# Sparse attention followed by a squared-ReLU MLP: exponentials become the stationary operand of the second attention product

## The chip, the core and the metric

The kernel runs on one core of a Trainium2 chip. The core has a matrix engine (TensorE; "PE" in the profile, and "PEld" for its weight loads), a vector engine (VectorE, "DVE"), a scalar engine for activation functions (ScalarE, "ACT"), a general engine (GpSimd, "POOL") and a sync engine ("SP") that here only issues DMA transfers. The metric is the device time of one execution in microseconds (us). The median of three runs of the kernel before is 309.66 us, from 307.91 to 309.68.

A matrix product on TensorE has two operands. The stationary one is loaded into the array by a weight load (LDWEIGHTS); its columns become the rows (partitions) of the result. The moving one is then streamed through, and its columns become the columns of the result. The result is summed up in PSUM[...].

## The reference, cut to what matters

There are 4 batches, 8 heads, 768 positions and 64 numbers per head. A query block of 32 positions sees its neighbours, the first and last block, and three drawn blocks; all else is masked. The heads of one position, put side by side, are the 512 inputs of the MLP.

```python
scores = scale * np.matmul(q, k.transpose(0, 1, 3, 2))
scores = np.where(mask, scores, -1000000000.0)
scores = scores - np.max(scores, axis=-1, keepdims=True)
attn = np.exp(scores)
attn = attn / (np.sum(attn, axis=-1, keepdims=True) + 1e-09)
out = np.matmul(attn, v)
# ... heads side by side: x is (3072, 512)
h = x @ w_in               # (512, 2048)
r = np.maximum(h, 0.0)
return (r * r) @ w_out     # (2048, 512)
```

## The kernel before

Two heads form a pair, u, so there are 16 of them, four for each batch. Queries are taken 256 at a time (qi, three of them) and keys 256 at a time (cp, three of them). One step of attention is therefore (u, qi, cp), and there are 16 x 3 x 3 = 144 steps. Scores are computed transposed, with keys on the partitions and queries along the row; ACT takes the exponential of 1024 of them per partition in one instruction; DVE multiplies by the mask (116 steps; in the first 28 the mask is added in the scores by TensorE).

The second product has the values as its stationary operand. Each of the two value tiles has 64 columns of one head and 64 columns of ones, so the result holds, by feature, the sum over the values in one half of the partitions and the sum of the exponentials, 64 times over, in the other half:

```python
def values(u, qi, cp):
    ...
    otile[u, qi] = pool.tile([P, 2, QW], F32, name="po", tag=tag)      # QW = 256
    for c in range(2):
        nc.tensor.matmul(po[:, 0, :], VA[i][:, n, :], pT[:, 0, c, :], start=first, stop=last, ...)
        nc.tensor.matmul(po[:, 1, :], VB[i][:, n, :], pT[:, 1, c, :], start=False, stop=last, ...)
```

When the three cp of a (u, qi) are in, the sums are inverted, by ACT as exp(-ln(sum)) for 44 of the 48, by DVE for four, and DVE multiplies. The result already lies by feature, as the MLP needs it (xT):

```python
def inverse(u, qi, on="ACT"):
    ...
        nc.scalar.activation(out=ls[0:D, :], in_=po[D:P, 0, :], func=AF.Ln)
        nc.scalar.activation(out=ls[D:P, :], in_=po[0:D, 1, :], func=AF.Ln)
        nc.scalar.activation(out=rs, in_=ls, func=AF.Exp, scale=-1.0)
    # ... or on DVE: two copies and a reciprocal

def normalize(u, qi):
    ...
    V.tensor_mul(out=xT[b][0:D, a, qsl], in0=po[0:D, 0, :], in1=rs[0:D, :])
    V.tensor_mul(out=xT[b][D:P, a, qsl], in0=po[D:P, 1, :], in1=rs[D:P, :])
```

The MLP takes 256 positions at a time in the first batch and 384 in the others. Its first product (hidden, tile ph) is followed by ReLU on DVE or ACT and squaring on GpSimd, its second (output, tile py) by a copy and a store:

```python
def hidden(T, f, half):      # w is 256 or 384 positions
    ...
        nc.tensor.matmul(ph, w_in_sb[:, kc, f * P:(f + 1) * P], xT[b][:, kc, c0:c0 + w], ...)
def output(T, ts, part):
    ...
        nc.tensor.matmul(py, gtile[T, f][:, ts * P:(ts + 1) * P], w_out_sb[:, f, :], ...)
```

The order of all this on the engines is fixed when the program is built. A small scheduler in the kernel holds a list of tasks, each with an engine (or a choice of two), a cost in us written by hand, a priority, what it waits for and what buffer it takes; it plays them through and writes each engine's instructions in the order in which they came out. At run time each engine works off its own list in order. The MLP of one batch is mixed in this way into the attention of the next.

```python
va = Task("PE", 0.44, k + 2.2, (lambda a=a: values(*a)), deps=[mm] + cv[u] + va_all[-1:], ...)
if cp == CP - 1:
    on = {"ACT": (1.2, k - 9)}
    if u < HP and qi < NQ_REC:
        on["DVE"] = (2.6, k - 9)
    inv = Task(on, 0, 0, (lambda *on, u=u, qi=qi: inverse(u, qi, *on)), deps=[va], **SEM)
    mu[u, qi] = Task("DVE", 0.87, k - 9, (lambda u=u, qi=qi: normalize(u, qi)), deps=[inv], ...)
```

Of the kernel before, what the change touches and what calls it, by code (L numbers as in the profile page):

```python
# [19 lines left out]
P = 128  # L20
# [5 lines left out]
def kernel(  # L26
# [8 lines left out]
    out: bass.AP,  # L35
):


# [141 lines left out]

    sb_i = consts.tile([nb, n_rand * 2], I32, name="sb_i")
    nc.sync.dma_start(out=sb_i, in_=sampled_blocks.bitcast(I32))
    load_part(nc.scalar, 0, 1, 0, 1)
    load_part(nc.scalar, 0, 0, 0, 1)
    load_part(nc.sync, 0, 1, 1, CP)
# [10 lines left out]
    V, G = nc.vector, nc.gpsimd  # L196
    QT, KT, VA, VB = [], [], [], []
    NPB = 5
    for i in range(NPB):
        QT.append(consts.tile([P, S], BF, name=f"QT{i}"))  # L200
        KT.append(consts.tile([P, S], BF, name=f"KT{i}"))
        VA.append(consts.tile([P, NCH, P], BF, name=f"VA{i}"))
        VB.append(consts.tile([P, NCH, P], BF, name=f"VB{i}"))

    def init_v(eng, i):
        eng.memset(VA[i][:, :, D:P], 1.0)
        eng.memset(VB[i][:, :, 0:D], 1.0)

# [35 lines left out]
    def one_hot_b(n0, n1):  # L244
        cols = slice(n0 * P, n1 * P)
        V.tensor_copy(out=oh[HALVES[1], cols], in_=oh[HALVES[0], cols])
# [14 lines left out]
                    op0=AOP.min, op1=AOP.min)  # L261
    V.memset(oh[HALVES[0], 2 * P:], 1.0)
    V.memset(pm[:, 0, 0:1], 0.0)
    V.memset(pm[:, 0, nb - 1:nb], 0.0)
    one_hot(2, NCH)
    bm = consts.tile([nb, 2, D], BF, name="bm")
# [7 lines left out]
    V.scalar_tensor_tensor(out=bm[:, :, 0:nb], in0=pm[:, 1:2, :].broadcast_to([nb, 2, nb]), scalar=NEG,  # L274
                           in1=pm[:, 0:1, :].broadcast_to([nb, 2, nb]), op0=AOP.mult, op1=AOP.mult)


# [35 lines left out]
    def cast_v(u, h):  # L313
        dst = VB[u % NPB][:, :, D:P] if h else VA[u % NPB][:, :, 0:D]
        G.tensor_copy(out=dst, in_=raw[u][2][:, h])  # L315

# [7 lines left out]

    def evac(u, w, c0, c1):
        dst = (KT if w else QT)[u % NPB]
        cols = slice(c0 * 2 * P, c1 * 2 * P)
        V.tensor_copy(out=dst[:, cols], in_=ptp.pop((u, w, c0))[:, cols])

# [27 lines left out]
    added = set()  # L357
    ptile, stile, otile, rtile, xT = {}, {}, {}, {}, {}

# [31 lines left out]
    def values(u, qi, cp):  # L391
        i = u % NPB
        pT = ptile.pop((u, qi, cp))
        if cp == 0:
            pool, tag = (ps_y, "y") if o_pool(u, qi) == "y" else (ps_o, "po")
            otile[u, qi] = pool.tile([P, 2, QW], F32, name="po", tag=tag)
        po = otile[u, qi]
        for c in range(2):
            n = cp * 2 + c
            first, last = n == 0, n == NCH - 1  # L400

            nc.tensor.matmul(po[:, 0, :], VA[i][:, n, :], pT[:, 0, c, :],  # L402
                             start=first, stop=last, skip_group_check=True)
            nc.tensor.matmul(po[:, 1, :], VB[i][:, n, :], pT[:, 1, c, :],  # L404
                             start=False, stop=last, skip_group_check=True)

    def inverse(u, qi, on="ACT"):
        po = otile[u, qi]
        ls = work.tile([P, QW], F32, name="ls", tag="ls")
        rs = work.tile([P, QW], F32, name="rs", tag="rs")  # L410
        if on == "ACT":
            nc.scalar.activation(out=ls[0:D, :], in_=po[D:P, 0, :], func=AF.Ln)  # L412
            nc.scalar.activation(out=ls[D:P, :], in_=po[0:D, 1, :], func=AF.Ln)  # L413
            nc.scalar.activation(out=rs, in_=ls, func=AF.Exp, scale=-1.0)  # L414
        else:
            V.tensor_copy(out=ls[0:D, :], in_=po[D:P, 0, :])
            V.tensor_copy(out=ls[D:P, :], in_=po[0:D, 1, :])
            V.reciprocal(out=rs, in_=ls)
        rtile[u, qi] = rs

    def normalize(u, qi):
        b, a = divmod(u, HP)
        if b not in xT:
            xT[b] = consts.tile([P, HP, S], BF, name=f"xT{b}")
        po, rs = otile.pop((u, qi)), rtile.pop((u, qi))
        qsl = slice(qi * QW, (qi + 1) * QW)
        V.tensor_mul(out=xT[b][0:D, a, qsl], in0=po[0:D, 0, :], in1=rs[0:D, :])  # L427
        V.tensor_mul(out=xT[b][D:P, a, qsl], in0=po[D:P, 1, :], in1=rs[D:P, :])  # L428

# [74 lines left out]
    NQ_Y = 2  # L504
    NQ_REC = 2
    KR, KY = 0, 500
# [3 lines left out]
    K_PARTS = {0: [(0, 1), (1, CP)]}  # L510
    land_k = [(3.1, 4.7), (6.3,), (9.5,), (12.0,)]
    land_q = [(3.7, 15.0, 16.5), (6.8, 15.4, 16.9), (9.9, 15.8, 17.3), (12.4, 16.2, 17.7)]
    land_v = [8.4, 11.0, 13.5, 14.6]
# [19 lines left out]
    wu[-1].put.append(wu[0].bufs[0])  # L533
    oh_t = Task("DVE", 0.2, 0.3, (lambda: one_hot_b(2, NCH)), after=4.2, **SEM)
    for i in range(HP):
        Task("POOL", 0.8, 0, (lambda i=i: init_v(G, i)), after=4.5 + 2.6 * i)
    rc = []
    for qi in range(NQ):
        rp = Task("PE", 0.107, -7 if qi == 0 else 6 * qi - 6, (lambda qi=qi: rows_product(qi)), get="h",
                  deps=[oh_t] if qi else [], after=4.0 if qi == 0 else 7.0 * qi, **pe)  # L540
        rc.append(Task({"ACT": (0.37, -7 if qi == 0 else 300), "DVE": (0.3, 6 * qi - 6)}, 0, 0, (lambda on, qi=qi: rows_copy(qi, on)), deps=[rp], put=[rp], **SEM))
    for qi in range(NQ):
        for cp in range(CP):
            k = (qi - NQ_ADD) % NQ * CP + cp
            s = HP * CP * (NQ_ADD + k // CP) + k % CP - 6
            t = Task("PE", 0.27, s, (lambda a=(qi, cp): mask_product(*a)), deps=[rc[qi]],
                     get="h", after=20.0 + 2.0 * k if k < 3 else 52.0 + 2.0 * k, **pe)
            mk[qi, cp] = Task("DVE", 0.62, s, (lambda a=(qi, cp): mask_copy(*a)), deps=[t], put=[t], **SEM)

    def prepare_first(u):  # L550
# [4 lines left out]
        for w, c0, c1, at, s in parts:  # L555
            n = c1 - c0
            a = (u, w, c0, c1)
            on = "POOL" if c0 and not w else "ACT" if u == 0 and not c0 else "DVE"
            c = Task(on, 0.06 + {"DVE": 0.17, "POOL": 0.36, "ACT": 0.31}[on] * n, s - 6,
                     (lambda a=a, e={"DVE": V, "POOL": G, "ACT": nc.scalar}[on]: cast_qk(e, *a)), get="qc", after=at, **SEM)  # L560
            t = Task("PE", 0.15 * n, s - 5 - w, (lambda a=a: transp(*a)), deps=[c], get="h", put=[c], **pe)
            e = Task("DVE", 0.06 + 0.17 * n, s - 5, (lambda a=a: evac(*a)), deps=[t], put=[t], **SEM)
            tr[u].append(c)
            for i in range(c0, c1):
                ev[u][w, i] = e
# [9 lines left out]
    def prepare(u):  # L575
# [17 lines left out]
        if u < NPB:  # L593
            early = [Task("POOL", 0.8, s0 - 8, (lambda u=u: init_v(G, u)), after=29.0, **SEM)]
        cv[u] = [Task("POOL", 0.6, s0 - 12, (lambda u=u, h=h: cast_v(u, h)), deps=[ld_t] + old_va + early, **SEM)
# [10 lines left out]
    def attend(s, slots):  # L606
        sc = Task("PE", 0.645 if len(slots) > 1 else 0.56 if s < N_ADD else 0.42, s, (lambda: scores(slots)),
                  deps=[t for u, qi, cp in slots if (u, qi, cp) in added for t in (rc[qi], oh_t)[:1 + (cp > 0)]] + [ev[u][1, cp] for u, qi, cp in slots] + [ev[u][0, qi] for u, qi, cp in slots] + sc_all[-1:],
                  get="ps", n=len(slots), **pe)
        sc_all.append(sc)  # L610
        for j, a in enumerate(slots):
# [4 lines left out]
            if a not in added:  # L616
                mm = Task("DVE", 0.82, k - 1, (lambda a=a: mask_mul(V, *a)), deps=[ex, mk[qi, cp]], **SEM)
            va = Task("PE", 0.44, k + 2.2, (lambda a=a: values(*a)), deps=[mm] + cv[u] + va_all[-1:],
                      get=None if cp else o_pool(u, qi), put=[ex], **pe)
# [3 lines left out]
            if cp == CP - 1:  # L623
                on = {"ACT": (1.2, k - 9)}
                if u < HP and qi < NQ_REC:
                    on["DVE"] = (2.6, k - 9)
                inv = Task(on, 0, 0, (lambda *on, u=u, qi=qi: inverse(u, qi, *on)), deps=[va], **SEM)
                mu[u, qi] = Task("DVE", 0.87, k - 9, (lambda u=u, qi=qi: normalize(u, qi)), deps=[inv],
                                 put=[va_all[-CP]], **SEM)

# [14 lines left out]
    for k, T in enumerate(TILES + [None]):  # L645
# [4 lines left out]
        for _, kind, x in sorted(both, key=lambda e: e[:2]):  # L650
# [14 lines left out]
            else:  # L665
# [12 lines left out]
                elif part == NY - 1:  # L678
# [3 lines left out]

    run_schedule({"PE": 3.3, "DVE": 3.9, "ACT": 3.1, "POOL": 4.4, "SP": 10.5},
                 {"ps": 2, "po": 1, "h": 2, "y": 1, "pT": PT_BUFS, "r": R_BUFS, "g": G_BUFS, "ys": 3,
                  "qc": QC_BUFS}, ring={"SP": 16.0, "POOL": 14.0})

# [29 lines left out]
```

The softmax here doesn't subtract the row's maximum and nothing guards it: scores larger than these inputs give would overflow.

## Time and profile before

| | before |
|---|---|
| median of three runs | 309.66 us |
| span of the profiled run | 306.4 us |
| TensorE matmuls | 2308, busy 97% of the span |
| VectorE | 393 instructions, busy 72% |
| ScalarE | 344 instructions, busy 71% |
| GpSimd | 226 instructions, busy 58% |
| granted TensorE clock | 1.00 |
| DMA | 34.47 MB, 112 GB/s in the mean |

The profile comes as a page with six parts: busy time of each engine; the span in 40 slices; the DMA queues; the chain of work that ended last; groups of instructions with their count, total and mean time and the idle time in front of them; and DMA issues. Further views list instructions in order of time, or the busy time of every engine in stretches of the span.

One thing has to be known to read the TensorE rows. Matmuls are pipelined: the time of one in a group ("mean ns") runs from its start to its end in the array, and the next one starts long before that. What a matmul costs is the distance from its start to the next one's start, and this is read from the list in order of time.

In slices, the run has three stages: from 7 to 37 us there is attention alone; from 37 to 260 us attention and MLP together; from 260 us to the end MLP alone.

### The profile page before, as it was taken

Reading aid. Unit: us, or ns where it says so; the run is one execution under the profiler, and the core shown is the slowest. Engines: PE = TensorE matmul, PEld = TensorE weight load, DVE = VectorE, ACT = ScalarE, POOL = GpSimd, SP = SyncE. Lnnn points to the kernel's source line nnn. Section 1 sums busy time; section 2 is a strip of 40 time slices with the busy share of each in tenths; the row PEclk is TensorE's granted clock in tenths of the full one; section 3 lists DMA queues with packets and bytes.
Section 4 is the critical chain, followed back from the end, with each engine's and each line's share of the span. In section 5 each row is a group of like instructions: output and inputs, shape, how many; then the busy total and the mean of one; then the engine's idle time right before and its main releaser. Section 6 shows DMA issues by size and latency. Waiting matters only on the chain.

```text
span 306.4 us, 6104 instructions
## 1 busy us (share of the span) xinstructions
PE 298.0 (97%) x2308; PEld 175.8 (57%) x2308; DVE 221.4 (72%) x393; ACT 218.8 (71%) x344; POOL 177.2 (58%) x226
## 2 busy tenths in 40 slices
PE   6999999999999999999999999999999999999995
PEld 4665656656766665555565555555655656555542
DVE  8778888698998878897767677767767866544521
ACT  3899999777978887888888888788888886200000
POOL 5680388765795576977444395755435345566620
PEclk9999999999999999999999999999999999999999
DMA  6997999735717167557001266501000000100002
GB/s 211 350 203 132 312 160 178 195 91 178 214 27 214 38 207 206 111 157 216 34 0 37 70 198 202 100 1 36 34 0 36 1 36 34 36 35 34 36 37 100
DMA packets 42597, 34.47 MB, mean 112 GB/s; under 512 B 20680, under 2 KB 39624, under 8 KB 42568
## 3 DMA queue, kind: packets, MB, share of 16 engines
q1 hardware_dynamic: 37656, 29.50, 34.1%
q0 software_dynamic: 4224, 4.19, 8.6%
q10 hardware_dynamic: 688, 0.39, 0.4%
q8 instruction: 18, 0.29, 0.4%
q14 instruction: 11, 0.09, 0.1%
HBM read 27.26 MB, written 6.29 MB: 109 GB/s over the span
## 4 chain that ended last, share of the span: by engine, by line
PE 85%; DVE 6%; ACT 4%; DMA 2%; issue 1%; POOL 0%; SPq 0%; ACTq 0%; DVEq 0%
PE py L471 25%; PE ph L444 24%; PE po L402 11%; PE ps L373 10%; PE po L404 9%; PE ps L369 3%; ACT pT L379 2%; DVE pT L384 2%; DMA ks<-in_k_dram 2%; PE pq L294 1%; PE pt L321 1%; DVE r L452 1%; DVE xT L428 1%; DVE xT L427 1%; ACT ls L413 1%
## 5 line engine op out<-in xcount | busy, mean ns | idle before, releaser
L458 POOL TENSOR_TENSOR g<-r 128x384 bf16<-128x384 f32 (+1 forms) x144 | 133.1, 935 | 89.1 <-DVE r L452 69.9
L379 ACT ACTIVATE pT<-ps 128x1024 bf16<-128x1024 f32 x144 | 142.4, 1019 | 16.3 <-PE ps L373 15.8
L384 DVE TENSOR_TENSOR pT<-pT,mask 128x1024 bf16<-128x1024 bf16 x116 | 93.1, 814 | 23.5 <-ACT pT L379 21.7
L444 PE MATMUL ph<-xT,w_in_sb 128*128 128x384 bf16 (+1 forms) x576 | 106.1, 308 | 0.1
L471 PE MATMUL py<-w_out_sb,g 128*128 128x512 bf16 x384 | 104.2, 379 | 0.5 <-ACT ys L478 0.5
L444 PEld LDWEIGHTS <-w_in_sb 128*128 128x128 bf16 x576 | 54.8, 98 | 38.6 <-issue 4.5
L402 PE MATMUL po<-pT,VA 128*128 128x256 bf16 x288 | 68.8, 274 | 0.9 <-DVE xT L428 0.7
L452 DVE TENSOR_SCALAR r<-ph 128x384 f32<-128x384 f32 (+1 forms) x96 | 48.8, 510 | 27.1 <-PE ph L444 17.2
L404 PE MATMUL po<-pT,VB 128*128 128x256 bf16 x288 | 68.2, 273 | 0.0
L471 PEld LDWEIGHTS <-g 128*128 128x128 bf16 x384 | 36.6, 98 | 29.0 <-issue 3.2
L373 PE MATMUL ps<-QT,KT 64*128 64x256 bf16 x576 | 46.8, 271 | 0.3 <-ACT pT L379 0.3
L402 PEld LDWEIGHTS <-VA 128*128 128x128 bf16 x288 | 28.0, 97 | 19.0 <-issue 10.2
L373 PEld LDWEIGHTS <-KT 64*128 64x128 bf16 x576 | 23.2, 94 | 21.0 <-issue 17.6
L404 PEld LDWEIGHTS <-VB 128*128 128x128 bf16 x288 | 28.2, 98 | 5.4 <-issue 0.9
L450 ACT ACTIVATE r<-ph 128x384 f32<-128x384 f32 (+1 forms) x48 | 21.9, 456 | 12.5 <-PE ph L444 10.8
L478 ACT COPY ys<-py 128x512 f32<-128x512 f32 x15 | 8.7, 580 | 28.9 <-PE py L471 28.9
L427 DVE TENSOR_TENSOR xT<-po,rs 64x256 bf16<-64x256 f32 x48 | 19.7, 410 | 9.8 <-ACT rs L414 9.5
L412 ACT ACTIVATE ls<-po 64x256 f32<-64x256 f32 x44 | 16.8, 381 | 11.1 <-PE po L404 10.2
L309 POOL CAST qc<-qs 128x768 bf16<-128x768 f32 (+1 forms) x20 | 15.2, 767 | 10.4 <-DMA qs<-in_q_dram 9.1
L428 DVE TENSOR_TENSOR xT<-po,rs 64x256 bf16<-64x256 f32 x48 | 20.5, 428 | 0.6
L414 ACT ACTIVATE rs<-ls 128x256 f32<-128x256 f32 x44 | 18.3, 417 | 1.4
L315 POOL CAST VA<-vs 128x384 bf16<-128x384 f32 x16 | 9.3, 584 | 15.2 <-DMA vs<-in_v_dram 9.5
(57 smaller groups left out, 123.9 us busy)
## 6 DMA issues: line engine op xcount, KB each, us to landing
vs<-in_v_dram SPq DMA_DIRECT2D x16, 384.0 KB, 5.0
out_dram<-ys SPq DMA_DIRECT2D x23, 256.0 KB, 2.1
ks<-in_k_dram SPq DMA_DIRECT2D x15, 384.0 KB, 4.3
qs<-in_q_dram SPq DMA_DIRECT2D x12, 384.0 KB, 3.6
w_in_sb<-in_moe_w_in_dram POOLq DMA_DIRECT2D x4, 512.0 KB, 8.0
w_out_sb<-in_moe_w_out_dram POOLq DMA_DIRECT2D x4, 512.0 KB, 11.1
qs<-in_q_dram SPq DMA_DIRECT2D x11, 128.0 KB, 5.1
ks<-in_k_dram SPq DMA_DIRECT2D x1, 256.0 KB, 4.0
```

Of the source, the lines that this page charges most:

```text
L373: nc.tensor.matmul(ps[:, h, c, :], KT[i][hs, ksl[c]], QT[i][hs, qsl], start=not add, stop=True, skip_group_check=True)
L379: nc.scalar.activation(out=pT, in_=stile.pop((u, qi, cp)), func=AF.Exp, scale=scale)
L384: eng.tensor_mul(out=pT, in0=pT, in1=mask[:, None, qi, cp * 2:cp * 2 + 2, :].broadcast_to([P, 2, 2, QW]))
L402: nc.tensor.matmul(po[:, 0, :], VA[i][:, n, :], pT[:, 0, c, :], start=first, stop=last, skip_group_check=True)
L404: nc.tensor.matmul(po[:, 1, :], VB[i][:, n, :], pT[:, 1, c, :], start=False, stop=last, skip_group_check=True)
L427: V.tensor_mul(out=xT[b][0:D, a, qsl], in0=po[0:D, 0, :], in1=rs[0:D, :])
L428: V.tensor_mul(out=xT[b][D:P, a, qsl], in0=po[D:P, 1, :], in1=rs[D:P, :])
L444: nc.tensor.matmul(ph, w_in_sb[:, kc, f * P:(f + 1) * P], xT[b][:, kc, c0:c0 + w], start=(kc == 0), stop=(kc == KM - 1))
L450: nc.scalar.activation(out=r, in_=htile.pop((T, f)), func=AF.Relu)
L452: V.tensor_scalar(out=r, in0=htile.pop((T, f)), scalar1=0.0, scalar2=None, op0=AOP.max)
L458: G.tensor_mul(out=g, in0=r, in1=r)
L471: nc.tensor.matmul(py, gtile[T, f][:, ts * P:(ts + 1) * P], w_out_sb[:, f, :], start=(f == 0), stop=(f == NF - 1))
```

## The change

The two operands of the second attention product change places. The exponentials, 128 queries at a time, become the stationary operand, and the values of one head with one column of ones, 65 columns in all, become the moving one. The result then lies by query: for each of its 128 partitions 64 sums of values and, in column 64, the sum of the exponentials. The division needs one number per query and head, so the inverse is a small reciprocal on DVE and no longer exp(-ln) on ACT. In exchange the result lies the wrong way round for the MLP and has to be transposed: by TensorE for the first batch (12 of the 48 tiles, with a copy out of PSUM), by a DMA transpose for the others (36). The purpose is to stream fewer columns through TensorE (8 x 65 in place of 4 x 256 for each step; half of the stationary columns of before were ones), and to take the inverses from ACT and the wide multiplications from DVE.

With this go smaller edits at the start: the value tiles need only two columns of ones (before 64), the loads and the one-hot tile of the mask are issued in another order, and two copies of the first tiles may run on ACT.

```diff
@@ values
-            nc.tensor.matmul(po[:, 0, :], VA[i][:, n, :], pT[:, 0, c, :],
-                             start=first, stop=last, skip_group_check=True)
-            nc.tensor.matmul(po[:, 1, :], VB[i][:, n, :], pT[:, 1, c, :],
-                             start=False, stop=last, skip_group_check=True)
+            for h in range(2):
+                for j in range(QW // P):
+                    nc.tensor.matmul(po[:, j, h, :], pT[:, h, c, j * P:(j + 1) * P], VV[i][:, n, h, 0:D + 1],
+                                     start=n + h + j == 0, stop=n == NCH - 1, skip_group_check=True)
@@ inverse, normalize
-            nc.scalar.activation(out=ls[0:D, :], in_=po[D:P, 0, :], func=AF.Ln)
-            nc.scalar.activation(out=ls[D:P, :], in_=po[0:D, 1, :], func=AF.Ln)
-            nc.scalar.activation(out=rs, in_=ls, func=AF.Exp, scale=-1.0)
...
-        V.tensor_mul(out=xT[b][0:D, a, qsl], in0=po[0:D, 0, :], in1=rs[0:D, :])
-        V.tensor_mul(out=xT[b][D:P, a, qsl], in0=po[D:P, 1, :], in1=rs[D:P, :])
+        V.reciprocal(out=rs, in_=po[:, :, D])
+        V.tensor_tensor(out=xn, in0=po[:, :, 0:D], in1=rs[:, :, None].broadcast_to([P, QW // P * 2, D]), op=AOP.mult)
@@ new
+    def x_transp(u, qi):
+        xn = xtile.pop((u, qi)).rearrange("p (j h) d -> p j (h d)", h=2)
+        pt = ps_h.tile([P, QW], BF, name="px", tag="h")
+        for j in range(QW // P):
+            nc.tensor.transpose(pt[:, j * P:(j + 1) * P], xn[:, j, :], identb)
+    def x_evac(u, qi, on):
+        (nc.scalar.copy if on == "ACT" else V.tensor_copy)(out=x_to(u, qi), in_=xtile.pop((u, qi)))
+    def x_dma(u, qi):
+        nc.sync.dma_start(out=x_to(u, qi).rearrange("r (n p) -> r n p", p=P),
+                          in_=xtile.pop((u, qi)).rearrange("p g d -> p (g d)"), transpose=True)
@@ attend
-            va = Task("PE", 0.44, k + 2.2, (lambda a=a: values(*a)), deps=[mm] + cv[u] + va_all[-1:],
+            va = Task("PE", 0.42, k + 2.2, (lambda a=a: values(*a)), deps=[mm] + cv[u] + va_all[-1:],
...
+                nm = Task("DVE", 0.55, k - 9, (lambda u=u, qi=qi: normalize(u, qi)), deps=[va],
+                          get="xn", put=[va_all[-CP]], **SEM)
+                if u < HP:
+                    xp = Task("PE", 0.12, k - 9, (lambda u=u, qi=qi: x_transp(u, qi)), deps=[nm], ...)
+                    mu[u, qi] = Task({"DVE": (0.3, k - 9), "ACT": (0.37, k - 9)}, 0, 0, ... x_evac ...)
+                else:
+                    mu[u, qi] = Task("SP", 1.3, k - 9, (lambda u=u, qi=qi: x_dma(u, qi)), deps=[nm],
+                                     put=[nm], late=2.0, dma=0.4)
```

## The prediction

> **What bounds the kernel now.** I read the page's busy times and chain of waits first, then the groups, then the busy times of the three stages, and last the matmuls in order of time.
>
> ```profile
> PE 298.0 (97%) x2308; PEld 175.8 (57%) x2308; DVE 221.4 (72%) x393; ACT 218.8 (71%) x344; POOL 177.2 (58%) x226
> ...
> PE 85%; DVE 6%; ACT 4%; DMA 2%; issue 1%; POOL 0%; SPq 0%; ACTq 0%; DVEq 0%
> ```
>
> TensorE is the bound: 85% of the chain that ended last. The three stages, each with the busy time of every engine:
>
> ```profile
> 7.00:37.00 30.00, 29.62 (x341) 18.78 (x337) 23.61 (x50) 27.49 (x36) 13.09 (x28) 1.00 1.00 248
> 37.00:260.00 223.00, 221.19 (x1724) 132.55 (x1722) 174.78 (x293) 185.18 (x297) 138.50 (x158) 1.00 0.42 106
> 260.00:302.00 42.00, 42.00 (x222) 21.61 (x221) 17.00 (x30) 3.42 (x7) 21.11 (x26) 1.00 0.12 45
> ```
>
> After the length come PE, PEld, DVE, ACT and POOL. In the first stage ACT is full too (27.5 of 30); in the middle one DVE stands at 78% and ACT at 83%; the last is TensorE alone. The groups that the change touches:
>
> ```profile
> L384 DVE TENSOR_TENSOR pT<-pT,mask 128x1024 bf16<-128x1024 bf16 x116 | 93.1, 814 | 23.5 <-ACT pT L379 21.7
> L402 PE MATMUL po<-pT,VA 128*128 128x256 bf16 x288 | 68.8, 274 | 0.9 <-DVE xT L428 0.7
> L404 PE MATMUL po<-pT,VB 128*128 128x256 bf16 x288 | 68.2, 273 | 0.0
> L427 DVE TENSOR_TENSOR xT<-po,rs 64x256 bf16<-64x256 f32 x48 | 19.7, 410 | 9.8 <-ACT rs L414 9.5
> L412 ACT ACTIVATE ls<-po 64x256 f32<-64x256 f32 x44 | 16.8, 381 | 11.1 <-PE po L404 10.2
> L414 ACT ACTIVATE rs<-ls 128x256 f32<-128x256 f32 x44 | 18.3, 417 | 1.4
> ```
>
> A matmul's 274 ns is its passage, not its cost. The cost is the distance between starts, here from the list in order of time, TensorE's matmuls and then two of its weight loads:
>
> ```profile
> 11.12 0.27 PE L402 MATMUL po<-pT,VA 128*128 128x256 bf16 x1
> 11.23 0.27 PE L404 MATMUL po<-pT,VB 128*128 128x256 bf16 x1
> 11.34 0.61 PE L321 MATMUL pt<-identb,qc 128*128 128x128 bf16 x8
> 11.78 0.27 PE L402 MATMUL po<-pT,VA 128*128 128x256 bf16 x1
> ```
>
> ```profile
> 9.05 0.11 PEld L321 LDWEIGHTS <-qc 128*128 128x128 bf16 x2 [0.21 <-issue]
> ```
>
> A value product of 256 columns costs 0.11 us (11.12 to 11.23; over a run of twelve it is 0.109). Eight transposes of 128 columns, each with a new full stationary operand, take from 11.34 to 11.78, 0.055 us each (0.056 where the starts are read one by one). And two weight loads, each 0.10 long by itself, fit in 0.11 us: the second starts some 0.015 us after the first. So a weight load holds up the stream far less than its own duration says.
>
> **What the Trainium skill says.** (1) "TensorE: Matmul & The Clock Gate", section "LDWEIGHTS (loading the stationary operand)", gives columns / 1.2 ns, 107 ns for 128 columns. The record agrees as a duration (97 to 98 ns) but not as a cost: pairs of load and product run here every 56 ns. (2) The same page, "Back-to-back issue gap", gives columns / 2.4 + 2.5 ns for a lone product, a floor near 25 ns, and some 81 ns for each product of 128 columns in a stream of load and product pairs. The trace agrees with the first (0.109 at 256 columns, 0.056 at 128) and contradicts the 81. No run here goes below 128 columns. (3) "PSUM — Partial Sum Buffer", "Specifications (TRN2)": cache lines of 8 bytes, and patterns that aren't contiguous slow matmuls. The new results are 65 fp32 wide, so every second one starts in mid line; no run here shows what that costs. (4) "VectorE: DVE Perf Modes", "The perf-mode tier table": a two-tensor operation with an operand in PSUM runs at the lowest rate. The trace agrees: 256 elements from PSUM take 0.41 us.
>
> **The change part by part.**
>
> *Value products.* Removed: 576 x 0.109 = 62.8 us of TensorE. Added: 144 x 8 = 1152 products of 65 columns. The line through 0.109 at 256 and 0.056 at 128 has 0.41 ns per column and 3 ns fixed, 0.030 us at 65 (an estimate; the load's 0.015 hides under it): 34.6 us. Saved 28.2.
>
> *Transposes by TensorE.* 12 tiles x 2 x 0.056 = 1.3 us. Net for TensorE: -26.9.
>
> *ACT.* Off go 44 x (0.381 + 0.376 + 0.417) = 51.7 us.
>
> *DVE.* Off go 48 x (0.410 + 0.428) = 40.2, and the four inverses there, 4 x (0.426 + 0.417 + 1.752) = 10.4. On come 48 multiplications of 256 elements from PSUM at 0.42 (as the ReLU of 128x256) and 48 reciprocals of 4 elements (0.13 estimated: the smallest operations here take that, and 1752 ns for 256 leave 27 for 4), 26.4 in all, and nine copies at 0.27, 2.5. The scheduler then gives DVE 80 ReLUs of 384 in place of 63, and 27 of 256 in place of 33, net +7. DVE: about -15.
>
> *GpSimd and SP.* 36 DMA transposes come to SP. Those of Q and K, three times as large, need 1.2 us to issue and 2.9 to land; tasks after them wait in SP's order.
>
> *Where it lies.* The built instruction order says how the work is cut. Before the first hidden product there are now 54 x 4 = 216 value products of the new kind, 27 steps (before 23); behind the last value product stand 204 hidden and 200 output products (before 96 and 122). So the tail grows, and the middle must be summed anew:
> - First stage. ACT needs 27 x 1.02 = 27.5 us for its exponentials from 7.4 on and is now the bound, as TensorE falls to about 0.86 a step: scores 0.43, two switches between the 64-row scores and 128-row products at some 0.1 each, values 0.24. It ends near 37.5.
> - Middle, before 223.5 us. Off: 108 hidden at 0.163, 17.6; 78 outputs at 0.216, 16.8; 32 score products at 0.054, 1.7; values from 484 x 0.109 = 52.8 to 936 x 0.030 = 28.1, 24.7. On: 0.4. TensorE needs 163.
> - But DVE, counted in the same way over its order, needs 158 there (115 masks x 0.814 = 94, 39 divisions 21, ReLUs 27, casts 9, mask copies, stores and evacuations 7), ACT 134. Two engines with nearly the same load, in fixed orders, don't overlap fully; with 6% for waits I take 172.
> - Tail: 204 x 0.163 + 200 x 0.216 = 76.5, and 3.7 from the last product to the end as before.
> Sum 37.5 + 172 + 76.5 + 3.7 = 289.7 of span. The median was 3 us above the profiled span before: 292 us.
>
> **Rivals.** *A. A floor near 52 ns for each pair of load and product* (the load itself, the feed of instructions, or the half cache lines). For it: nothing in the trace runs below 0.055, and the new code's hand-written cost is 0.42 for eight. Against it: the two loads 0.015 apart. Then values cost 59.9, the net saving is 1.6, the middle takes about 183 and is TensorE-bound again, the first stage 40: some 304 to 306 us. *B. DVE becomes the bound of the middle stage and runs with more waits than I gave it*: it has 158 of work, and its masks (0.81 in the mean) reach 1.1 to 1.2 us beside GpSimd. At 185 for the middle: 305. *C. The detour by DMA transposes.* Each batch's MLP now waits for a landing, behind loads of 384 KB and stores in SP's order; six tiles of MLP with 2 us each would give back 12: 304. Against it: the other batches' work lies ready, and the single PSUM tile of the sums is free after one DVE step of 0.55 us, which before took 1.17 on ACT and 0.84 on DVE. *D. All hidden*: if DVE and TensorE interleave perfectly, 281.
>
> **Range and chances.** The main line, at 0.030 to 0.038 a product, I hold at two in three, with 283 to 298; A at one in five; the rest is B and C on top. Predicted 292 us, range 282 to 307. Faster by over 2% (below 303.5): 0.77; within: 0.19; slower: 0.04, as no computing engine gets more work than it sheds.
>
> **What would show it.** The distance between starts in a run of eight value products: 30 ns (right), 50 and more (A). The middle stage's busy times: DVE over 90% with TensorE waiting for masks speaks for my middle; TensorE full there speaks for A. Hidden products waiting for a DMA of xT: C. The division as 0.42 + 0.13, a tail of about 76 us behind the last value product, and the first hidden product near 37. I am wrong if the products follow at 50 ns or above, or if TensorE stands idle over 20 us in the middle.

## The result and the profile after

The change makes the kernel faster, and by about as much as was predicted: 296.31 us in the median (294.70 to 298.01 in four runs) beside 309.11 (307.91 to 309.68) for the kernel before. The ratio is 0.959, with a 95% interval from 0.952 to 0.966. The profiled span went from 306.4 to 292.8 us.

First the page of the kernel after: its busy times and the engines' shares of the chain that ended last.

```profile
PE 275.7 (94%) x2870; PEld 160.5 (55%) x2908; DVE 208.2 (71%) x400; ACT 166.8 (57%) x206; POOL 173.6 (59%) x223
...
PE 59%; DVE 20%; DMA 10%; issue 4%; ACT 2%; SPq 2%; POOL 2%; DVEq 0%; ACTq 0%; POOLq 0%
```

(38 of TensorE's 2908 matmuls, all of them output products, have no record in this trace, so its 94% is a little low.) ACT lost 52.0 us and DVE 13.2. TensorE is still the busiest engine, but its share of the chain fell from 85% to 59%, DVE's rose from 6% to 20%, and that of DMA, mostly loads of K and V, from 2% to 10%. Where this happens is seen in the busy times by stage, cut at the starts of the first hidden product, of the last value product and of the last product of all (start and end, length, then PE, PEld, DVE, ACT, POOL, granted clock, DMA share, GB/s):

```profile
7.00:39.05 32.05, 31.65 (x514) 21.04 (x513) 17.56 (x51) 28.09 (x30) 13.48 (x26) 1.00 1.03 249
39.05:212.24 173.19, 163.04 (x1939) 97.47 (x1968) 154.13 (x273) 131.24 (x163) 113.74 (x129) 1.00 0.56 139
212.24:288.37 76.13, 75.71 (x402) 39.47 (x407) 32.51 (x58) 4.11 (x7) 42.89 (x52) 1.00 0.12 43
```

In the middle stage TensorE now stands idle for 10.1 us of 173.2 (before 1.8 of 223.0), DVE is busy for 89% (before 78%), and ACT has dropped from 83% to 76%. The waits of this stage say for whom TensorE stands idle (engine, line, released by: us in total, times, longest):

```profile
PEld L402 <- DVE pT L383: 12.9, 29, 1.2
PEld L402 <- DVE xn L410: 7.7, 13, 1.3
PE po L402 <- DVE pT L383: 4.6, 14, 0.7
PE po L402 <- DVE xn L410: 2.6, 6, 0.8
```

All four are value products waiting for DVE: for a masked tile of exponentials, or for the division that frees the one PSUM tile of the sums (po). The rows of PEld and PE tell in part of the same waits and aren't added. The 10.1 us count only the time in which no matmul is on its way; where the distances between starts exceed what the products cost elsewhere, TensorE loses some 14 us in this stage (an estimate from all its starts; the same sum is about 4 before). TensorE waits for no load here; DVE waits 2.4 us and GpSimd 4.8 for loads of K and V, and what these cost the whole wasn't tested. No hidden product waits for a landing of xT; the view has no such line.

How cheap the products became is read from TensorE's instructions in order of time:

```profile
122.95 0.42 PE L402 MATMUL po<-VV,pT 128*128 128x65 bf16 x8 [0.26 <-DVE pT L383]
123.22 0.49 PE L447 MATMUL ph<-xT,w_in_sb 128*128 128x384 bf16 x2
```

Eight value products, each with its own weight load, start at 122.95, and the next group follows at 123.22: 0.27 us for eight (0.26 in the median of all steps). Within the groups the distance from one start to the next is 32 ns in the median. The 0.42 behind the start is the passage of the group: seven distances of 0.032 and the last product's own 0.194. Last, the groups that the prediction priced:

```profile
L383 DVE TENSOR_TENSOR pT<-pT,mask 128x1024 bf16<-128x1024 bf16 x116 | 99.3, 878 | 5.6 <-ACT pT L378 5.1
L402 PE MATMUL po<-VV,pT 128*128 128x65 bf16 x1152 | 58.7, 194 | 7.7 <-DVE pT L383 4.6
L410 DVE TENSOR_TENSOR xn<-po,rs 128x256 bf16<-128x256 f32 x48 | 20.4, 424 | 1.7
L409 DVE RECIPROCAL rs<-po 128x4 f32<-128x4 f32 x48 | 8.5, 176 | 9.7 <-PE po L402 9.6
```

The multiplication came as estimated (0.424 for 0.42). The masks, which the change doesn't touch, take 0.878 in place of 0.814, and the reciprocal 0.176 in place of 0.13. The same two rows give the wait that is gone: before, DVE stood 21.7 us in front of the masks for ACT's exponentials, now 5.1.

### The profile page after: what moved, and what is told of

It reads as the page before. It is cut to its first block, busy times and chain, and to the rows that moved or that the text cites. A ratio compares the mean times of both kernels' runs of the same rounds, so it can differ in the third digit from the quotient of the medians.

```text
span 292.8 us, 7241 instructions
## 1 busy us (share of the span) xinstructions
PE 275.7 (94%) x2870; PEld 160.5 (55%) x2908; DVE 208.2 (71%) x400; ACT 166.8 (57%) x206; POOL 173.6 (59%) x223
## 4 chain that ended last, share of the span: by engine, by line
PE 59%; DVE 20%; DMA 10%; issue 4%; ACT 2%; SPq 2%; POOL 2%; DVEq 0%; ACTq 0%; POOLq 0%
PE py L474 20%; PE ph L447 20%; DVE pT L383 11%; PE po L402 8%; PE ps L372 6%; DMA ks<-in_k_dram 6%; DMA vs<-in_v_dram 3%; PE ps L368 2%; DVE xn L410 2%; DVE r L455 2%; ACT pT L378 2%; DVE qc L309 2%; DVE mask L299 1%; SPq L168 1%; PE pt L320 1%
## 5 line engine op out<-in xcount | busy, mean ns | idle before, releaser
L474 PE MATMUL py<-w_out_sb,g 128*128 128x512 bf16 x346 | 97.0, 379 | 1.8 <-issue 0.2
L455 DVE TENSOR_SCALAR r<-ph 128x384 f32<-128x384 f32 (+1 forms) x107 | 55.7, 521 | 40.4 <-POOL g L461 21.0
L402 PEld LDWEIGHTS <-pT 128*128 128x128 bf16 x1152 | 47.1, 98 | 37.2 <-DVE pT L383 12.9
L402 PE MATMUL po<-VV,pT 128*128 128x65 bf16 x1152 | 58.7, 194 | 7.7 <-DVE pT L383 4.6
L372 PEld LDWEIGHTS <-KT 64*128 64x128 bf16 x576 | 23.5, 95 | 17.6 <-issue 14.2
L314 POOL CAST VV<-vs 128x384 bf16<-128x384 f32 x32 | 21.4, 698 | 13.8 <-DMA vs<-in_v_dram 12.4
L453 ACT ACTIVATE r<-ph 128x256 f32<-128x256 f32 (+1 forms) x37 | 15.9, 431 | 11.5 <-PE ph L447 10.2
L410 DVE TENSOR_TENSOR xn<-po,rs 128x256 bf16<-128x256 f32 x48 | 20.4, 424 | 1.7
L409 DVE RECIPROCAL rs<-po 128x4 f32<-128x4 f32 x48 | 8.5, 176 | 9.7 <-PE po L402 9.6
L309 DVE CAST qc<-ks 128x768 bf16<-128x768 f32 (+1 forms) x16 | 11.6, 724 | 3.5 <-DMA ks<-in_k_dram 3.5
L368 PE MATMUL ps<-bq,oh 64*128 64x256 bf16 x112 | 11.7, 288 | 0.4 <-ACT pT L378 0.4
```

What stands on the lines that cost most here:

```text
L309: (eng.copy if eng is nc.scalar else eng.tensor_copy)(out=c[:, ns], in_=raw[u][w][:, :, ns, :].rearrange("p t n d -> p n t d"))
L314: G.tensor_copy(out=VV[u % NPB][:, :, h, 0:D], in_=raw[u][2][:, h])
L368: nc.tensor.matmul(ps[:, h, c, :], oh[hs, ksl[c]], bq[hs, qsl], start=c == 0, stop=False, skip_group_check=True)
L372: nc.tensor.matmul(ps[:, h, c, :], KT[i][hs, ksl[c]], QT[i][hs, qsl], start=not add, stop=True, skip_group_check=True)
L402: nc.tensor.matmul(po[:, j, h, :], pT[:, h, c, j * P:(j + 1) * P], VV[i][:, n, h, 0:D + 1], start=n + h + j == 0, stop=n == NCH - 1, skip_ ...
L410: V.tensor_tensor(out=xn, in0=po[:, :, 0:D], in1=rs[:, :, None].broadcast_to([P, QW // P * 2, D]), op=AOP.mult)
```

## Experiments

Two theories were to be told apart. The first: the gain is TensorE's cheaper products, it needed ACT's relief as well, and what limits the middle stage now is DVE, mostly through its masks. The rival: TensorE's new pairs of load and product are still the limit, by a floor or by waits that the detour through transposes brings. All changes below are made to the kernel after, ratios are to the kernel before, and the times of stages are from the profiled run.

### Wider moving operand

```diff
-    nc.tensor.matmul(po[:, j, h, :], pT[...], VV[i][:, n, h, 0:D + 1],
+    w0 = (n * 2 + h) * (D + 2)
+    nc.tensor.matmul(po[:, j, h, :], pT[...], VV[i].rearrange("p n h d -> p (n h d)")[:, w0:w0 + P],
```

128 columns are streamed where 65 are needed; the extra ones are neighbours in the tile and aren't read (tiles are widened to hold them).

> The same kernel with 128 moving columns in place of 65 (the other 63 are streamed and never read); order and all other engines unchanged. A product should then cost 0.056 in place of 0.030 us, 1152 x 0.026 = 30 us more on TensorE, 24 of them in the middle stage. Theory 1 (the saved columns are the gain; TensorE had some 10 us of slack against DVE in the middle): middle about 173 + 14 = 187 us, first stage 41, time 313 or so, no faster than the kernel before. Theory 2 (the gain comes from the work taken from ACT and DVE, TensorE's columns hardly matter): time stays below 303.

Measured: ratio 1.006 (1.002 to 1.009), median 314.15 us of eleven runs. Six of them ran in a slower state of the chip and are not in the ratio; the other five have a median of 310.36. One step's products in order of time, and the middle stage:

```profile
101.25 0.61 PE L404 MATMUL po<-VV,pT 128*128 128x128 bf16 x8
```

```profile
42.85:229.88 187.03, 183.99 (x1969) 120.67 (x1968) 153.12 (x270) 130.96 (x163) 111.44 (x126) 1.00 0.50 125
```

The distance is 56 ns in the median, as the transposes of before had shown for 128 columns. That is 1152 x 0.024 = 28 us more for TensorE, and the span grew by 17.6: the rest fell into TensorE's waits, whose idle time shrank from 10.1 to 3.0 us in this stage. The whole gain of the change is gone, though ACT and DVE keep theirs. So the gain hangs on the products' 32 ns, and this kernel shows what a floor in the fifties would have cost.

### ACT's old work put back

```diff
+    nc.scalar.activation(out=ls[0:D, :], in_=warm[0:D, :], func=AF.Exp)
+    nc.scalar.activation(out=ls[D:P, :], in_=warm[0:D, :], func=AF.Exp)
+    nc.scalar.activation(out=lr, in_=ls, func=AF.Exp, scale=-1.0)
```

Each division is accompanied by three activations of the sizes of the old inverse, on a constant; nobody reads them. The built order doesn't know of them. They sum to 59.5 us, 7.8 more than the old inverses, since there are 48 in place of 44 and two of the three activations take longer (0.41 for 0.38).

> The change with ACT's old load put back: at each of the 48 divisions ACT runs three activations of the sizes of the old inverse on a constant tile; nothing reads them. Adds 48 x 1.17 = 56 us to ACT, 46 of them in the middle stage. Theory 1 (TensorE's columns alone are the gain, ACT had room): within 1% of the changed kernel, 296. Theory 2 (both reliefs are needed, because the steps now come faster than ACT with its inverses could serve them): ACT has 127 + 46 = 173 us in a middle of 173 and 9 to 11 us more in the first stage, so the middle goes to 180 to 185 and the time to 310 to 318, and the gain is gone.

Measured: ratio 1.011 (1.006 to 1.015), median 311.8 us. The first and the middle stage:

```profile
7.00:43.82 36.82, 31.29 (x512) 21.30 (x508) 18.14 (x54) 35.51 (x54) 15.30 (x34) 1.00 0.99 237
43.82:229.40 185.58, 168.90 (x1969) 98.26 (x1968) 150.49 (x270) 169.83 (x282) 106.01 (x126) 1.00 0.50 126
```

ACT is the fullest engine in both (35.5 of 36.8, 169.8 of 185.6), its share of the chain is 34% (2% in the kernel after), and TensorE, with its cheap products, stands idle for 16.7 us in the middle. Even if the 7.8 us are taken off in full, less than half of the gain is left. Taking work from TensorE alone would have brought little in this order or nothing; both reliefs were needed. An order planned with these activations in it wasn't tried and might do better.

### Narrower moving operand

```diff
+    d0 = 0 if n == 0 else D + 1 - 32
-    nc.tensor.matmul(po[:, j, h, :], pT[...], VV[i][:, n, h, 0:D + 1],
+    nc.tensor.matmul(po[:, j, h, d0:], pT[...], VV[i][:, n, h, d0:D + 1],
```

For all but the first of the six key tiles only 32 of the 65 columns are streamed: the sums of the other 33 features are left incomplete.

> Five of the six key tiles stream only 32 of the 65 columns of the values (the sums of the other 33 features are left incomplete); order and the other engines unchanged. Takes up to 5/6 x 1152 x 33 x 0.41 ns = 13 us from TensorE, 11 of them in the middle stage, unless a product cannot go below some 25 ns. Theory 1 (DVE bounds the middle stage): the time stays within 1% of 296. Theory 2 (TensorE's columns still set the pace, its waits are only where the order puts them): 284 to 288.

Measured: 296.16 us, ratio 0.958 (0.954 to 0.962): the time of the kernel after. One step's products, then the middle stage:

```profile
101.15 0.36 PE L403 MATMUL po<-VV,pT 128*128 128x32 bf16 x8
101.36 0.38 PE L448 MATMUL ph<-xT,w_in_sb 128*128 128x256 bf16 x2
```

```profile
38.90:212.60 173.70, 160.59 (x1969) 92.77 (x1968) 155.32 (x273) 130.94 (x163) 112.91 (x128) 1.00 0.56 139
```

The distance fell only to 25 ns in the median and 26 in the mean (0.21 for eight), so TensorE was relieved of some 960 x 0.006 = 6 us. That is less than half of what the columns would suggest, and the test is weaker for it; but these 6 us bought nothing (295.03 us in the run whose clock was 1.00, where the kernel after has 294.70 and 295.36). TensorE isn't what sets the middle stage. The Trainium skill, "TensorE: Matmul & The Clock Gate", section "Back-to-back issue gap", states an issue floor near 25 ns up to 64 columns; the 25 at 32 agrees, and its formula for a lone product gives 29.6 for 65 columns where the trace has 32. That floor lies below the change's width, and so rival A's doesn't exist at this one.

### Fewer masks

```diff
 def mask_mul(...):
+    if cp == 1:
+        return
```

39 of the 116 mask multiplications are left out; masked keys of the middle third are then counted in the output.

> The mask multiplication of DVE is left out where cp is 1 (some 39 of 116, so masked keys count there; order unchanged). Takes 39 x 0.88 = 34 us from DVE and nothing from TensorE. Theory 1 (DVE is the bound of the middle stage, 166 us busy of 173): the middle falls to what TensorE needs, 161 to 165, time 285 to 289. Theory 2 (TensorE's waits come from the fixed order and from round trips, not from DVE's load): middle stays at 171 or above, time 294 to 296.

Measured: 287.84 us, ratio 0.930 (0.925 to 0.935). The middle stage:

```profile
40.27:205.88 165.61, 161.46 (x1970) 98.93 (x1969) 122.04 (x234) 129.93 (x163) 103.06 (x129) 1.00 0.62 145
```

DVE's load in the stage fell by 32.1 us, the stage by 7.6, and then it met TensorE, which has only 4.2 us of idle time left there. DVE was the limit, but by a narrow margin.

### GpSimd made light

```diff
-    r = work.tile([P, TWM], F32, name="r", tag="r", bufs=R_BUFS)[:, 0:T[2]]
+    r = work.tile([P, TWM], BF, name="g", tag="g", bufs=G_BUFS + R_BUFS)[:, 0:T[2]]
-    G.tensor_mul(out=g, in0=r, in1=r)
+    g = rltile.pop((T, f))
+    G.tensor_mul(out=g[:, 0:32], in0=g[:, 0:32], in1=g[:, 0:32])
```

Why do the same masks take longer than before the change? In this version GpSimd squares 32 columns in place and leaves the others unsquared; the order on all engines is that of the kernel after.

> The changed kernel in its own order, with GpSimd's squaring cut to 32 of the 256 or 384 columns, in place in the tile that the ReLU writes (the other columns stay unsquared). Takes some 100 us of work from GpSimd, nothing from DVE, ACT or TensorE. Theory 1 (a mask multiplication on DVE takes longer while GpSimd works): the masks' mean falls from 0.88 to 0.76 or less, DVE has 14 us less to do in the middle stage, which shortens to 160 to 167, time 283 to 290. Theory 2 (the masks' length has nothing to do with GpSimd): mean stays at 0.85 or above and the time within 1% of 296.

Measured: 286.26 us, ratio 0.924 (0.919 to 0.929). The groups of the squares and of the masks, then the middle stage:

```profile
L460 POOL TENSOR_TENSOR g<-g 128x32 bf16<-128x32 bf16 x144 | 53.7, 377 | 139.4 <-DVE g L455 108.8
L383 DVE TENSOR_TENSOR pT<-pT,mask 128x1024 bf16<-128x1024 bf16 x116 | 82.1, 726 | 10.1 <-ACT pT L378 9.5
```

```profile
38.86:206.17 167.31, 161.77 (x1939) 100.01 (x1968) 135.98 (x273) 130.42 (x163) 67.56 (x130) 0.98 0.61 145
```

GpSimd's 173.6 us became 95.4, and DVE's 208.2 became 189.5 with no instruction fewer: its masks fell from 0.878 to 0.726, its casts of K from 0.724 to 0.592. (Its input is now a bf16 tile; the ReLUs that write it take 0.521 as before.) TensorE's weight loads wait 5.4 us for masks in place of 12.9, the middle stage is 5.9 us shorter, the span 6.1. (TensorE was granted only half its clock for 6.8 us of this stage, so without that the difference may be larger.) In the trace of the kernel after, the masks during which GpSimd was idle throughout take 0.69 us (16 of them), and those during which it worked throughout, on squares or on casts, 0.98 (36). The Trainium skill, "SBUF — State Buffer", section "Who interferes with whom", says that a DVE instruction with both inputs in SBUF contends with a GpSimd instruction that reads SBUF; the traces agree, and put a size on it.

### All transposes by TensorE

```diff
-                if u < HP:
+                if True:
```

> The 36 DMA transposes of the later batches are undone: TensorE transposes these tiles too, and DVE or ACT copies them out (16 more on DVE, 20 more on ACT), as for the first batch. Adds 36 x 2 x 0.056 = 4 us to TensorE and 16 x 0.28 = 5 us to DVE. Theory 1 (the DMA detour is hidden, DVE bounds the middle): 4 to 9 us slower than the change, 300 to 305. Theory 2 (hidden products lose time waiting for the DMA's landing): equal or faster, 290 to 296.

Measured: 296.58 us, ratio 0.960 (0.956 to 0.965). It was expected to be slower, and that was a miss. The middle stage:

```profile
39.77:211.29 171.52, 164.66 (x2022) 99.24 (x2021) 153.24 (x284) 136.59 (x184) 111.14 (x125) 1.00 0.52 125
```

The 72 further transposes and the copies out of PSUM find room (of the 48 copies ACT does 23 and DVE 25) in an order that is made anew: the middle stage is 1.7 us shorter, the tail 3.5 longer. The time is the same. So the DMA detour cost nothing that TensorE transposes would save, and saved nothing either.

### The true costs in the scheduler's book

```diff
-            va = Task("PE", 0.42, ...values...)
+            va = Task("PE", 0.24, ...values...)
```

The scheduler plans a value step at 0.42 us, as long as the passage of its eight products; 0.24 is eight times the prediction's 0.030, and the distances in the trace sum to 0.26.

> One number changed: the scheduler's cost of eight value products is 0.24 us, which is their distance from start to start, in place of 0.42, which is the passage of the eight. The order is made anew: more of the MLP goes into the middle stage (128 hidden and 146 output products behind the last value product in place of 204 and 200) and ACT gets more of the ReLUs there. Theory 1 (DVE bounds the middle, so attention can't go faster, but its waits can be filled with MLP work of TensorE): TensorE's idle time of some 20 us is used for half or more, time 282 to 290. Theory 2 (the order does not matter, DVE's load sets the end): within 1% of 296.

Measured: 292.31 us, ratio 0.945 (0.941 to 0.950). It is faster than the kernel after, but outside what was expected. The middle stage, and a stretch of DVE, GpSimd, TensorE and ACT near its start:

```profile
35.31:234.07 198.76, 192.81 (x2170) 112.49 (x2166) 166.73 (x285) 142.09 (x179) 134.91 (x151) 0.98 0.56 132
```

```profile
44.28 5.28 DVE L383 TENSOR_TENSOR pT<-pT,mask 128x1024 bf16<-128x1024 bf16 x4
...
45.77 3.24 POOL L461 TENSOR_TENSOR g<-r 128x256 bf16<-128x256 f32 x4
...
47.58 0.42 PE L402 MATMUL po<-VV,pT 128*128 128x65 bf16 x8 [1.47 <-DVE pT L383]
...
48.42 1.02 ACT L378 ACTIVATE pT<-ps 128x1024 bf16<-128x1024 f32 x1 [1.47 <-PE ps L372]
```

The tail behind the last value product is now 52.1 us in place of 76.1, so 24 us of MLP were brought forward; but the middle grew by 25.6. Four masks in a row take 5.28 us beside GpSimd's casts and squares, 1.32 each, where the plan had 0.82, and TensorE and through it ACT wait for them. So part of the gain went into a new wait. A second loss lies right behind: from 48.27 to 55.09 us TensorE was granted half its clock, and was busy for 5.60 us of that, so that up to 2.8 us are lost there. All four runs show a mean clock of 0.987 to 0.992, and without this loss the time could lie just within what was expected; how much of the miss is the masks' was not separated. The next run books all three costs near what the traces show (0.26, 0.92 and 0.60):

```diff
-            mm = Task("DVE", 0.82, ...mask_mul...)      va = Task("PE", 0.42, ...)      nm = Task("DVE", 0.55, ...)
+            mm = Task("DVE", 0.92, ...mask_mul...)      va = Task("PE", 0.24, ...)      nm = Task("DVE", 0.6, ...)
```

> As the run with 0.24 booked for eight value products, and besides 0.92 for a mask multiplication (measured there 0.92, booked 0.82) and 0.60 for a division (measured 0.176 + 0.424, booked 0.55). The order then gives DVE 89 ReLUs in place of 100. Theory 1 (DVE is the bound of the middle, and the order only has to know it): 2 to 5 us below 292, 287 to 290. Theory 2 (order worth nothing more): 291 to 294.

Measured: 286.02 us, ratio 0.924 (0.918 to 0.929), a little better than expected. The middle stage:

```profile
33.94:227.32 193.38, 190.35 (x2175) 113.69 (x2172) 163.09 (x282) 143.55 (x186) 138.84 (x152) 1.00 0.57 136
```

TensorE is full again (190.4 of 193.4), the tail is 50.7. Compared with the kernel after, the scheduler also gave ACT 15 more instructions and DVE 15 fewer, and no stretch of half clock falls in this stage; how much of the gain is due to these, and how much to the order, wasn't separated.

### Squares that ACT may take

```diff
-    sq_of[x] = Task("POOL", SQ[w][2], n_key, ...square...)
+    sq_of[x] = Task({"POOL": (SQ[w][2], n_key), "ACT": (SQ[w][1] - 0.07, n_key)}, 0, 0, ...square...)
```

This stands on top of the three true costs, and uses the room that the change has left on ACT: there `square` is an activation. ACT gets 80 of the 144 squares.

> As before in this batch, and the squaring of the MLP may also run on ACT (activation Square); the order gives ACT 80 of the 144. Takes some 70 us of work from GpSimd. In the change a mask multiplication takes 0.69 us where GpSimd is idle throughout and 0.98 where it works throughout. Theory 1 (GpSimd's work slows DVE's masks, and DVE bounds the middle): masks fall to 0.80 or less in the mean, 9 us or more off DVE, time 280 to 286. Theory 2 (masks are slow for another reason): masks stay near 0.9 and the time stays at that of the run without it.

Measured: 282.99 us (281.48 to 283.47), ratio 0.915 (0.911 to 0.919): the fastest version of all, 4.5% under the kernel after. Its page, the mask group and the middle stage are three views:

```profile
PE 273.6 (97%) x2908; PEld 160.8 (57%) x2908; DVE 193.9 (69%) x376; ACT 212.2 (76%) x310; POOL 106.8 (38%) x143
```

```profile
L383 DVE TENSOR_TENSOR pT<-pT,mask 128x1024 bf16<-128x1024 bf16 x116 | 94.1, 835 | 5.5 <-ACT pT L378 5.3
```

```profile
34.88:234.55 199.67, 198.61 (x2222) 117.75 (x2219) 156.92 (x280) 170.94 (x253) 90.58 (x101) 1.00 0.56 134
```

TensorE is at 97% of the span, and idle for 1.1 us in the middle. The masks' mean of 0.835 isn't as low as expected. Taken one by one they are as in the kernel after: 0.69 where GpSimd is idle (42 masks, there 16) and 1.03 where it works throughout (26, there 36); only the mix moved. The order moved too: the tail is 42.1 us in place of 50.7, the middle 6.3 longer, and what the masks brought apart from that wasn't separated. The intervals of this version and of the last overlap a little (0.918 to 0.919), so it is likely and not certain that this step brought something.

## Why the prediction was right

**Value products.** The line through two measured widths gave 0.030 us for 65 columns; the trace has 0.032, which is some 37 us for all, so that about 26 us were saved where 28.2 were predicted. This was the step on which all hung, and the wider operand shows it: at 56 ns nothing is left of the gain. Rival A falls. The sign for it that the prediction named, the hand-written 0.42 for eight, equals the passage of a group and not its cost. The half cache lines, on which the prediction could cite a warning but no run, cost nothing visible: the distances behind the third to eighth product of a group are 33, 29, 33, 29, 33 and 29 ns, and only the fifth and sixth of these write from the start of a line.

**ACT and TensorE's transposes.** ACT lost 52.0 us. The 51.7 of the prediction are the inverses alone; 11 ReLUs fewer took off 6 us more, a few copies came on, and less of its work overlaps, so the close agreement is luck. That ACT's relief mattered was in the prediction only as a lower count; with the work put back, ACT is the fullest engine, and the gain is gone.

**First stage.** Its end at 39.05 was predicted near 37.5. The sum shown, 27 exponentials from 7.4 on, ends at 34.9, and no term is given for the rest; in the trace 29 start before the first hidden product, the first at 8.17. ACT is busy for 28.09 us of 32.05 and waits 2.8 us for scores between its exponentials, while TensorE's records cover 31.65: that ACT alone is the bound here isn't shown. The smaller edits at the start weren't tested apart.

**Middle.** 173.2 for 172. TensorE's 163.0 for 163 is luck in part: the row lacks some records, and it counts passages where the prediction counted costs. DVE was mis-sized: the terms "115 masks x 0.814" and 0.13 for a reciprocal are 0.878 and 0.176, some 8 and 2 us, so the sum of its instructions there is 168 and not 158. (The 154.1 of the stage's row count instructions that overlap only once; at 89% they stay just under the sign of 90% that the prediction named.) It didn't harm the total, since the 6% for waits covered it; that was luck too. The light squares show that the 0.878 hangs on GpSimd. Not more squares than before stand beside the masks (52.4 us of their time before, 51.7 after), but more of GpSimd's casts do (9.2 and 17.6 us). Beside GpSimd a mask takes 0.98 us for 0.69, so the 8.4 us more should cost some 2.5 us (an estimate), a third of the rise; the rest stays open.

**Rival B** was right in the mechanism and wrong in the size: DVE does limit the stage, as the missing masks (-7.6 us) and the narrower operand (no change) show together, but TensorE stands idle for 10 us there, and B's 185 would have meant some 22. **Rival C** isn't there: no hidden product waits for a landing, and without the detour the time is the same. **Rival D** (281, all hidden) is what a better order comes near to: span 282.4 with the three costs put right, 281.0 with the squares on ACT as well, in a different cut of stages.

**Tail and end.** 76.1 for 76.5, and 4.4 from the start of the last product to the end of the run (4.0 from its end, for 3.7). The sum, 292.8 of span for 289.7, was 3.1 too low, of which the first stage is 1.6, the middle 1.2 and tail and end together 0.3. The median stands 3.5 above it, for the 3 that were added.

## What to carry to other kernels

Price a matrix product by the distance between starts, and price it so in any hand-written plan too: the passage of a short group is 1.6 times its cost here, and with costs near the measured ones nearly the same instructions ran 3.5% faster. Count every engine stage by stage before relieving one: here TensorE's relief alone would have been worth little or nothing without ACT's, and what both freed ended at DVE. An instruction whose time depends on what another engine does beside it (masks and squares) has to be planned at its loaded time, and it may be cheaper to move the other engine's work than to shorten one's own.

## What the runs showed of the hardware

A pair of weight load (128 columns) and product costs 56 ns with 128 moving columns, 32 with 65 and 25 with 32, in the median: the load, 98 ns by its own record, is hidden down to there. A mask over 128x1024 bf16 takes 0.69 us alone, 0.98 to 1.03 in the mean beside a working GpSimd, and 1.3 in the worst stretch shown. A reciprocal of 128x4 from PSUM takes 0.176 us, and the multiplication of 128x256 behind it 0.424. The 36 small DMA transposes land 2.5 us after their issue in the median, and it made no difference to the time whether they or TensorE did the work.
